# A dynamic convolution and two dense layers on one core: block 0 shared by heads, weights corrected on VectorE, boot order changed

## The chip, the cores and the metric

The kernel runs on 1 core of one Trainium2 chip. The metric is the device time of one execution in microseconds (us). It is given as the median of several runs; a profile is one further execution with its own time.

## What is computed

`x` is (2, 4096, 192) in f32, `weight_gen` is (2, 4096, 8 heads, 7 taps). The weights of the two dense layers are f64 numbers.

```python
w = softmax(weight_gen, axis=taps)                 # + 1e-9 in the sum
x_pad = six zero rows + x                          # per batch, along the sequence
a[b,s,h,g] = sum_k w[b,s,h,k] * x_pad[b,s+k,h,g]   # 8 heads x 24 columns
for (w_in, w_out), gate in ((moe, elu), (moe2, hardswish)):
    a = gate(a @ w_in) @ w_out                     # 192 -> 2048 -> 192, 8192 rows
```

## The kernel before, in words

The 8192 rows lie as 128 partitions of 64 positions. A **block** is four positions of every partition, 512 rows; there are 16, and each goes through both layers (m = 0 and 1). A **cell** (m, i, q) is one block and one eighth of the 2048 hidden columns. Cells run in one list, 256 of them, in a software pipeline: in step n, PE runs the first product of cell n (`first_product`) and the second product of cell n-3 (`second_product`), ACT the exponential (L494, L495) and the rounding to fp32r (L501), DVE the gate (L511, L514) and the rounding's remainder (L505). Every product is made of three, high by high, high by low and low by high, so weights and activations are each kept as a rounded high part and a low part. The two halves of the partitions (k = 0, 1) run as two streams of 64-row products on PE; a note on SP's queue tells one stream when the other has left a bank.

**Boot.** Cells 0 to 15 are blocks 0 and 1 of the first layer, in the order of `SPLIT`: columns 0 to 4 of both blocks, then 5 to 7 of both. While they run, the first layer's weights are made, in 16 **units** (class `Unit`), sorted by the cell that first needs them. Units 0 to 3, 5 and 10 to 12 are columns of the layer's first matrix (kind "i"), needed from cells 0, 1, 2, 3, 4, 10, 11, 12 on; units 4, 6 to 9 and 13 to 15 are rows of its second (kind "o"), needed in cells 3 to 7 and 13 to 15. The f64 words arrive in a raw buffer; `begin` (ACT, L150) and `s0` to `s3` (DVE, L154 to L169) build the f32 value `f` from the high word, `s4` (DVE, L182) the part from the low word, `high` (ACT, L175) the rounded weight. `p5` makes the low part on PE: identity times `f`, minus identity times the rounded weight, plus identity times the low word's part (L187 to L189), and `p6` (ACT, L194) evicts it. Units below 6 are `busy`: their steps work on a PSUM bank. The list `at` names the step in which a unit's DVE steps are issued, `high` follows one step later and `p5`, `p6` two. Unit n's raw buffers are asked for by `want` up to two units ahead. After the boot the second layer's units are made by `wst`.

**Convolution.** `attention(i)` gives the steps for block i: softmax (`s0` to `s2`, L246 to L272; DVE, the exponential on ACT) and seven products with six sums. For block 0 DVE takes positions 0 and 1 (its products and weights in PSUM) and GpSimd (POOL) positions 2 and 3; later blocks are POOL's alone. Six rows of halo ahead of each partition's positions come from the partition before, in two DMAs of 63 partitions (L226), requested after the first unit's weights, which `load_block` requests through `between`. `prepare` transposes the result on PE (L327, L331), casts it to its high part on ACT (L338), subtracts on DVE (L340), and copies halves of the partitions across by four DMAs (L345).

**The end of a block.** `fold_b` and `fold_a` collect the second product; blocks 0 and 1, whose columns are split, keep a first sum (`keep_b`) that DVE adds in `rest` (L369) before the halves are added (L373).

**DMAs.** All are issued on SP. `later` issues one at once or puts it on a list, `transfers` issues from that list behind the notes in `matmuls`; before cell 16 the list is emptied after every cell's products.

Of the kernel before, what the change touches and what calls it, by code (L numbers as in the profile page):

```python
# [17 lines left out]
def kernel(  # L18
# [26 lines left out]
    P = 128  # L45
# [29 lines left out]
    plus, minus = (cpool.tile([P, P], F32R, name=n) for n in ("plus", "minus"))  # L75
# [25 lines left out]
    def load_w(kind, m, q):  # L101
        raw = stage.tile([P, UN, 2], U32, tag="raw", name="raw", bufs=RAWS)
        if kind == "i":
            for k in range(2):
                c = (2 * q + k) * 2 * P
                src = w_in[m][:, c:c + 2 * P].rearrange("(g p) c -> p g c", p=HP)
                dst = raw[half[k]].rearrange("p (g c) b -> p g (c b)", g=3)
                if k == 0:
                    later(0, dst, src)
                else:  # L110
                    for s, g in enumerate((1, 0, 2)):
                        later(0, dst[:, s], src[:, g])
# [11 lines left out]
    class Unit:  # L124
# [52 lines left out]
        def s4(self):  # L177
            f = o = self.r.bitcast(F32)
            if self.m == 0:
                c = self.n % NQ * UN  # L180
                o = self.rr = bootr[:, c:c + UN]
            nc.vector.scalar_tensor_tensor(o, self.lw, 2.0**-52, f, op0=ALU.mult, op1=ALU.mult)  # L182

        def p5(self):

            hi, _, v = self.parts()
            nc.tensor.matmul(self.ps, ident, self.f.bitcast(F32), start=True, stop=False)  # L187
            nc.tensor.matmul(v(self.ps), minus, hi, start=False, stop=False)
            nc.tensor.matmul(self.ps, plus, self.rr, start=False, stop=True)  # L189
# [22 lines left out]
    def load_block(i, between=None):  # L212
        t0 = TM * i
        xt = xw.tile([P, TM + HALO, D], F32, tag="xt", name="xt", bufs=2)
        wt = xw.tile([P, TM * H, K], F32, tag="wt", name="wt", bufs=2)
        later(
            0, wt.rearrange("p a k -> p (a k)"), wv[:, t0:t0 + TM, :].rearrange("p t c -> p (t c)"))
        m = max(0, HALO - t0)
        later(0, xt[:, m:HALO + TM, :], xv[:, t0 - HALO + m:t0 + TM, :])
        if between:  # L220
            between()
        if m:

            for b in range(B):
                nc.gpsimd.memset(xt[b * PB:b * PB + 1, 0:m, :], 0.0)
                nc.sync.dma_start(  # L226
                    xt[b * PB + 1:(b + 1) * PB, 0:m, :],
                    xv[b * PB:(b + 1) * PB - 1, TP + t0 - HALO:TP + t0 - HALO + m, :])
        return xt, wt

    def attention(i):
# [6 lines left out]
        hn = n // 2  # L238
# [18 lines left out]

        if i == 0:

            pw = hset[1][0][:, 0:hn * K].rearrange("p (a k) -> p a k", k=K)  # L260
            po = hset[0][0][:, 0:2 * D].rearrange("p (t e) -> p t e", e=D)
            hs = [(nc.vector, slice(0, 2), pw, po), (nc.gpsimd, slice(2, 4), w3[:, hn:, :], tmp[:, 0:2])]
        else:
            hs = [(nc.gpsimd, slice(0, TM), w3, tmp)]

        def s2():
            s = tt["m"]
            if i == 0:
                v.tensor_tensor(pw, w3[:, :hn, :], s[:, :hn, :].to_broadcast([P, hn, K]), op=ALU.mult)
                v.tensor_tensor(w3[:, hn:, :], w3[:, hn:, :], s[:, hn:, :].to_broadcast([P, hn, K]), op=ALU.mult)  # L270
            else:
                v.tensor_tensor(w3, w3, s.to_broadcast(shp), op=ALU.mult)  # L272

        def product(k):
            def s():
                for eng, t, w, o in hs:
                    nt = t.stop - t.start
                    xk = xt[:, t.start + k:t.stop + k, :].rearrange("p t (h g) -> p t h g", g=G)
                    wk = w[:, :, k:k + 1].to_broadcast([P, nt * H, G])
                    if k == K - 1:  # L280
                        o = y[:, t, :]
                    eng.tensor_tensor(  # L282
                        o.rearrange("p t (h g) -> p t h g", g=G), xk,
                        wk.rearrange("p (t h) g -> p t h g", h=H), op=ALU.mult)
            return s

        def add():
            for eng, t, _, o in hs:
                eng.tensor_tensor(y[:, t, :], y[:, t, :], o, op=ALU.add)  # L289

        def add_a():
            for eng, t, _, o in hs:
                eng.tensor_tensor(y[:, t, 0:P], y[:, t, 0:P], o[:, :, 0:P], op=ALU.add)

        def add_d():

            for eng, t, _, o in hs:
                if t.stop - t.start == 2:
                    d = t.start // 2 * HP
                    eng.tensor_tensor(yd[:, :, d:d + HP], y[:, t, P:D], o[:, :, P:D], op=ALU.add)  # L300
                else:
                    v = lambda t: t.rearrange("p (a s) e -> p s a e", a=2)[..., P:D]
                    eng.tensor_tensor(yd.rearrange("p s (a e) -> p s a e", a=2), v(y), v(o), op=ALU.add)
# [11 lines left out]
    def prepare(m, i, parts=(0, 1)):  # L315
# [20 lines left out]
        def split():  # L336
# [6 lines left out]
            for k in "hl":  # L343
                for a in range(2):
                    later(first[m, i] == SPLIT if first[m, i] <= BOOT else 2, X[k][half[1 - a], 1].bitcast(F32), X[k][half[a], 0].bitcast(F32))  # L345
# [7 lines left out]
    def fold_b(m, i):  # L353
# [6 lines left out]
        if (m, i) in part:  # L360
            first_part = part.pop((m, i))
        else:
            first_part = None
# [3 lines left out]
        def rest():  # L367
            if first_part is not None:
                nc.vector.tensor_tensor(b, b, first_part, op=ALU.add)  # L369
# [42 lines left out]
    def first_product(n, k):  # L412
# [7 lines left out]
        for j, (w, x, s) in enumerate((  # L420
# [9 lines left out]
            c = q * UN + s * P  # L430
# [23 lines left out]
    def matmuls(n):  # L454
# [18 lines left out]
        for _, k, (o, w, r, st, sp, wait, tell) in sorted(plan, key=lambda e: e[:2]):  # L473
# [3 lines left out]
            if tell:  # L477
# [39 lines left out]
    RAWS, RB, YB = 4, 3, 1  # L517
# [4 lines left out]
    SPLIT = 5  # L522
    BOOT = EARLY = 2 * NQ
# [68 lines left out]
    def want(n):  # L592
        if n < len(units) and n not in made:
            u = made[n] = Unit(*units[n])
            u.n = n
            if n < BOOT:
                u.busy = n < 6

                u.bank = {1: acca[1], 2: accb, 3: acca[0], 5: acca[1]}.get(n, aux)

    def w_steps(n):
        def step(k):
            def s():
                if k < 0:
                    for a in range(3):
# [13 lines left out]
    with tc.manual_schedule():  # L619
# [5 lines left out]
        nc.scalar.mul(minus, ident, -1.0)  # L625
# [3 lines left out]
        for k in "aaaawwawawawaw":  # L629
# [15 lines left out]
        wst = Stream(wtasks)  # L645
        for n in range(len(cells) + LAG + 3):
# [49 lines left out]
            for i in range(2, NB):  # L696
# [13 lines left out]
            if n < BOOT:  # L710
# [33 lines left out]
```

## Time and profile before

| | |
|---|---|
| median of 3 runs | 1260.06 us (1259.47 to 1260.61) |
| the profiled execution | 1260.44 us |
| its span, first to last instruction | 1258.7 us |
| busy in the span | PE 1210.0, DVE 941.3, ACT 857.1, POOL 413.5 us |
| chain of work that ended last | PE 90%, DVE 5%, ACT 3%, DMA 1% |
| mean granted TensorE clock | 0.989 |

The span is shorter than the execution by what lies around it, 1.7 us. A busy time is a sum over the whole span; PE's matmuls are pipelined and their ends are modelled. Idle time of an engine is put down to what released it last. L345 is line 345 of the kernel above. In a timeline the first column is the start in us from the span's beginning, the second how long the instruction was on its engine; idle time before it stands in brackets with its releaser.

### The profile page before, as it was taken

Reading aid. Unit: us, or ns where it says so; the run is one execution under the profiler, and the core shown is the slowest. Engines: PE = TensorE matmul, PEld = TensorE weight load, DVE = VectorE, ACT = ScalarE, POOL = GpSimd, SP = SyncE. Lnnn points to the kernel's source line nnn. Section 1 sums busy time; section 2 is a strip of 40 time slices with the busy share of each in tenths; the row PEclk is TensorE's granted clock in tenths of the full one; section 3 lists DMA queues with packets and bytes.
Section 4 is the critical chain, followed back from the end, with each engine's and each line's share of the span. In section 5 each row is a group of like instructions: output and inputs, shape, how many; then the busy total and the mean of one; then the engine's idle time right before and its main releaser. Section 6 shows DMA issues by size and latency. Waiting matters only on the chain.

```text
span 1258.7 us, 25471 instructions
## 1 busy us (share of the span) xinstructions
PE 1210.0 (96%) x10176; PEld 1075.4 (85%) x10176; DVE 941.3 (75%) x1226; ACT 857.1 (68%) x1342; POOL 413.5 (33%) x234
## 2 busy tenths in 40 slices
PE   3997889999999999999999999999999999999998
PEld 2665778998999998999888888988888899999996
DVE  6879689899899999999777666666666666666663
ACT  2765678888888888888886565566656655666553
POOL 7425767777877777788000000000000000000000
PEclk9998989999999999999999999999999999999999
DMA  6341121122222212221111011111111111111110
GB/s 166 102 124 38 59 87 66 46 75 86 86 86 86 68 41 66 86 86 51 52 51 38 27 52 51 39 51 52 28 37 51 51 52 39 52 51 25 41 39 26
DMA packets 33686, 75.82 MB, mean 60 GB/s; under 512 B 4644, under 2 KB 17058, under 8 KB 33568
## 3 DMA queue, kind: packets, MB, share of 16 engines
q1 hardware_dynamic: 33568, 74.19, 20.2%
q8 instruction: 80, 1.31, 0.5%
q14 instruction: 38, 0.31, 0.1%
HBM read 36.43 MB, written 12.58 MB: 39 GB/s over the span
## 4 chain that ended last, share of the span: by engine, by line
PE 90%; DVE 5%; ACT 3%; DMA 1%; issue 1%; SPq 0%; DVEq 0%; ACTq 0%
PE h L474 41%; PE acca L474 28%; PE accb L474 19%; DVE gl L505 1%; ACT r L495 1%; ACT r L494 1%; DVE bootf L161 1%; DVE r L511 1%; DMA xt<-in_x_dram 1%; DMA xl<-xl 0%; DVE bootf L157 0%; DVE tr L169 0%; PE acca L327 0%; SPq L544 0%; DVE z L373 0%
## 5 line engine op out<-in xcount | busy, mean ns | idle before, releaser
L474 PE MATMUL h<-xh,wi_h 64*128 64x512 f32 x1536 | 574.2, 399 | 5.9 <-DVE r L511 3.2
L474 PE MATMUL h<-xh,wi_l 64*128 64x512 f32 x1536 | 574.8, 399 | 0.0
L474 PE MATMUL h<-xl,wi_h 64*128 64x512 f32 x1536 | 567.7, 398 | 2.0 <-DMA xl<-xl 2.0
L505 DVE TENSOR_TENSOR gl<-r,gh 128x1024 fp32r<-128x1024 f32 x256 | 374.8, 1464 | 64.7 <-ACT gh L501 61.7
L497 ACT ACTIVATE r<-h,three 128x512 f32<-128x512 f32 x256 | 176.6, 690 | 225.5 <-PE h L474 178.4
L474 PEld LDWEIGHTS h<-xh,wi_h 64*128 64x128 f32 x1536 | 287.1, 188 | 25.3 <-DVE r L511 4.9
L474 PEld LDWEIGHTS h<-xl,wi_h 64*128 64x128 f32 x1536 | 285.6, 188 | 19.4 <-DMA xl<-xl 3.0
L474 PEld LDWEIGHTS h<-xh,wi_l 64*128 64x128 f32 x1536 | 285.8, 188 | 16.7
L514 DVE SCALAR_TENSOR_TENSOR r<-r,h 128x512 f32<-128x512 f32 x256 | 176.1, 688 | 163.5 <-ACT r L497 162.6
L474 PE MATMUL acca<-gh,wo 64*128 64x512 f32 x1024 | 284.3, 397 | 0.0
L501 ACT CAST gh<-r 128x1024 fp32r<-128x1024 f32 x256 | 266.6, 1041 | 13.2 <-DVE r L511 12.4
L511 DVE SCALAR_TENSOR_TENSOR r<-r,h 128x512 f32<-128x512 f32 x256 | 174.1, 682 | 55.3 <-ACT r L495 54.6
L474 PEld LDWEIGHTS acca<-gh,wo 64*128 64x128 f32 x1024 | 191.5, 187 | 11.6
L282 POOL TENSOR_TENSOR tmp<-xt,wt 128x768 f32<-128x768 f32 (+1 forms) x96 | 188.8, 1966 | 7.4 <-DMA xt<-in_x_dram 1.2
L494 ACT ACTIVATE r<-h 128x512 f32<-128x512 f32 x256 | 152.7, 596 | 50.6 <-PE acca L474 26.9
L474 PE MATMUL accb<-gh,wo 64*128 64x512 f32 x512 | 165.6, 402 | 6.9 <-ACT wo L194 3.4
L495 ACT ACTIVATE r<-r 128x512 f32<-128x512 f32 x256 | 162.3, 634 | 8.1
L474 PE MATMUL accb<-gl,wo 64*128 64x512 f32 x512 | 163.0, 398 | 0.0
L474 PE MATMUL acca<-gl,wo 64*128 64x512 f32 x512 | 162.2, 396 | 0.0
L289 POOL TENSOR_TENSOR y<-y,tmp 128x768 f32<-128x768 f32 (+1 forms) x80 | 149.9, 1874 | 6.3
L474 PE MATMUL acca<-gh,wo1b 64*128 64x512 f32 x512 | 141.7, 396 | 0.3
L474 PE MATMUL acca<-gh,wo1a 64*128 64x512 f32 x512 | 140.3, 393 | 0.0
(143 smaller groups left out, 1850.3 us busy)
## 6 DMA issues: line engine op xcount, KB each, us to landing
xt<-in_x_dram SPq DMA_DIRECT2D x14, 960.0 KB, 5.4
xh<-xh SPq DMA_DIRECT2D x64, 192.0 KB, 2.7
xl<-xl SPq DMA_DIRECT2D x64, 192.0 KB, 2.9
raw<-in_moe_w_out_dram SPq DMA_DIRECT2D x16, 384.0 KB, 3.2
z<-z SPq DMA_DIRECT2D x16, 384.0 KB, 2.3
zin<-z SPq DMA_DIRECT2D x16, 384.0 KB, 3.0
out_dram<-ot SPq DMA_DIRECT2D x16, 384.0 KB, 2.3
raw<-in_moe_w_in_dram SPq DMA_DIRECT2D x16, 192.0 KB, 3.5
```

The source lines that it names most:

```text
L161: nc.vector.scalar_tensor_tensor(self.f, self.hw, 0xC0000000, self.b, op0=ALU.bitwise_and, op1=ALU.bitwise_or)
L282: eng.tensor_tensor(o.rearrange("p t (h g) -> p t h g", g=G), xk, wk.rearrange("p (t h) g -> p t h g", h=H), op=ALU.mult)
L289: eng.tensor_tensor(y[:, t, :], y[:, t, :], o, op=ALU.add)
L474: mm = nc.tensor.matmul(o, w, r, start=st, stop=sp).ins
L494: nc.scalar.activation(r, h, AF.Relu, scale=-1.0)
L495: nc.scalar.activation(r, r, AF.Exp, scale=-1.0)
L497: nc.scalar.activation(r, h, AF.Relu, bias=three)
L501: nc.scalar.copy(gg[n][0], rs[n])
L505: nc.vector.tensor_tensor(gl, rs.pop(n), gh.bitcast(F32), op=ALU.subtract)
L511: nc.vector.scalar_tensor_tensor(r, r, -1.0, h, op0=ALU.add, op1=ALU.max)
L514: nc.vector.scalar_tensor_tensor(r, r, 6.0, h, op0=ALU.min, op1=ALU.mult)
```

## The change

- `p5` has two products, both with the fp32r identity: one of `fl`, the other of the low word's part. `fl` is `f` minus the rounded weight, made by a new DVE step `left` one step after the unit's other DVE steps. The negative identity is gone. The low word's parts have four slots in place of eight, `fl` the other four.
- Block 0's convolution: DVE takes heads 0 to 4 of all four positions, POOL heads 5 to 7; POOL alone writes the last 64 columns.
- The halo's DMAs are issued before unit 0's weights. Block 0 is split (`prepare`) before the later softmax steps of block 1, not after them.
- Weight columns of the second half come in two DMAs in place of three, in another order, which `first_product` follows.
- `at` is written out: units 10 to 15 are made in steps 4, 5, 5, 6, 7, 8 in place of 5 to 10. Units 10 and 12 take the bank acca[1]. Raw buffers are five, and `want` looks three units ahead.
- From cell 3 on, DMAs of the boot go to the list and are issued up to three per cell behind the notes; the list is emptied at the ends of cells 0 to 2, 4 and 15. Block 1's half copies go to the front of the list, in turned order.
- The kept first sum is added in the step of `fold_b`, not in `fold_a`'s.

```diff
-    plus, minus = (cpool.tile([P, P], F32R, name=n) for n in ("plus", "minus"))
+    plus = cpool.tile([P, P], F32R, name="plus")
...
-                    for s, g in enumerate((1, 0, 2)):
-                        later(0, dst[:, s], src[:, g])
+                    later(0, dst[:, 0:2], src[:, 1:3])
+                    later(0, dst[:, 2], src[:, 0])
...
         def s4(self):
...
-                c = self.n % NQ * UN
+                c = self.n % 4 * UN
...
+                self.fl = bootr[:, c + 4 * UN:c + 5 * UN]
...
+        def left(self):
...
+            hi, _, v = self.parts()
+            nc.vector.tensor_tensor(v(self.fl), v(self.f.bitcast(F32)), hi.bitcast(F32), op=ALU.subtract)
...
         def p5(self):
...
-            hi, _, v = self.parts()
-            nc.tensor.matmul(self.ps, ident, self.f.bitcast(F32), start=True, stop=False)
-            nc.tensor.matmul(v(self.ps), minus, hi, start=False, stop=False)
+            nc.tensor.matmul(self.ps, plus, self.fl, start=True, stop=False)
...
-        if between:
-            between()
...
+        if between:
+            between()
...
-            pw = hset[1][0][:, 0:hn * K].rearrange("p (a k) -> p a k", k=K)
-            po = hset[0][0][:, 0:2 * D].rearrange("p (t e) -> p t e", e=D)
-            hs = [(nc.vector, slice(0, 2), pw, po), (nc.gpsimd, slice(2, 4), w3[:, hn:, :], tmp[:, 0:2])]
-        else:
-            hs = [(nc.gpsimd, slice(0, TM), w3, tmp)]
+            c = P // G
+            pw = hset[1][0][:, 0:TM * c * K].rearrange("p (t h k) -> p t h k", t=TM, k=K)
+            po = hset[0][0][:, 0:TM * c * G].rearrange("p (t h g) -> p t h g", t=TM, g=G)
+            hs = [(nc.vector, slice(0, c), pw, po), (nc.gpsimd, slice(c, H), w4[:, :, c:], th[:, :, c:])]
+        else:
+            hs = [(nc.gpsimd, slice(0, H), w4, th)]
+        yh = y.rearrange("p t (h g) -> p t h g", g=G)
...
          def product(k):
             def s():
+                for eng, h, w, o in hs:
+                    xk = xt[:, k:TM + k, :].rearrange("p t (h g) -> p t h g", g=G)[:, :, h]
+                    wk = w[:, :, :, k:k + 1].to_broadcast([P, TM, h.stop - h.start, G])
+                    eng.tensor_tensor(yh[:, :, h] if k == K - 1 else o, xk, wk, op=ALU.mult)
...
         def add_d():
...
+            v = lambda t: t.rearrange("p (a s) e -> p s a e", a=2)[..., P:D]
+            nc.gpsimd.tensor_tensor(yd.rearrange("p s (a e) -> p s a e", a=2), v(y), v(tmp), op=ALU.add)
...
-                    later(first[m, i] == SPLIT if first[m, i] <= BOOT else 2, X[k][half[1 - a], 1].bitcast(F32), X[k][half[a], 0].bitcast(F32))
+                    (later0 if first[m, i] <= BOOT else later)(2 - (first[m, i] == SPLIT), X[k][half[1 - a], 1].bitcast(F32), X[k][half[a], 0].bitcast(F32))
...
-            first_part = part.pop((m, i))
-        else:
-            first_part = None
+            p = part.pop((m, i))
+            jobs.append(lambda: nc.vector.tensor_tensor(b, b, p, op=ALU.add))
...
         def rest():
-            if first_part is not None:
-                nc.vector.tensor_tensor(b, b, first_part, op=ALU.add)
...
-            c = q * UN + s * P
+            c = q * UN + ((0, 2, 1)[s] if k else s) * P
...
-                if now >= BOOT and tell[1] == 1:
+                if now >= 3 and tell[1] == 1:
...
-        if now < BOOT:
+        if now < 3:
...
-    RAWS, RB, YB = 4, 3, 1
+    RAWS, RB, YB = 5, 3, 1
...
+    AT = (-3, -2, -1, 0, 0, 1, 1, 2, 3, 4, 4, 5, 5, 6, 7, 8)
...
-    now, waiting = None, []
+    now, waiting, jobs = None, [], []
...
-        if now is None or now >= len(cells) or now < BOOT and n == 0:
+        if now is None or now >= len(cells) or now < 3 and n == 0:
...
+    def later0(n, out, in_):
...
+        if now is None or n == 2:
+            nc.sync.dma_start(out, in_)
+        else:
+            waiting.insert(0, (now + n, out, in_))
...
-    at = []
-    for d, *_ in units:
-        at.append(min(d - 3, at[-1] + 1) if at else -3)
+    at = AT
+    assert all(a <= u[0] - 3 for a, u in zip(at, units))
...
-                u.bank = {1: acca[1], 2: accb, 3: acca[0], 5: acca[1]}.get(n, aux)
+                u.bank = {1: acca[1], 2: accb, 3: acca[0], 5: acca[1], 10: acca[1], 12: acca[1]}.get(n, aux)
...
     def w_steps(n):
         def step(k):
             def s():
...
-                    for a in range(3):
+                    for a in range(4):
...
-        for k in "aaaawwawawawaw":
+        for k in "aaaawwawawaw":
...
+        made[0].left()
...
-        for s in c1[:4]:
-            s()
-        prepare(0, 0)()
-        for s in c1[4:] + w_steps(1):
+        split = prepare(0, 0)
+        c1[0]()
+        split()
+        for s in c1[1:] + w_steps(1):
...
+        made[1].left()
...
+            for u in range(BOOT):
+                if at[u] == n - 1:
+                    made[u].left()
...
-            if n < BOOT:
+            if n < 3 or n == SPLIT - 1 or n == BOOT - 1:
...
```

## Rows read from the trace of the kernel before

**Rows 1.** Stages: us; busy PE, PEld, DVE, ACT, POOL; granted clock, DMA share, GB/s
```profile
23.70:50.00 26.30, 24.04 (x70) 16.28 (x70) 22.77 (x38) 16.12 (x31) 22.34 (x14) 1.00 0.58 172
50.00:86.70 36.70, 33.15 (x238) 24.45 (x240) 26.36 (x50) 26.79 (x51) 0.00 (x0) 1.00 0.36 105
86.70:127.10 40.40, 32.51 (x201) 22.45 (x200) 37.69 (x40) 22.29 (x42) 24.66 (x14) 0.87 0.17 55
127.10:171.50 44.40, 38.71 (x292) 31.44 (x294) 31.42 (x41) 27.12 (x44) 26.05 (x14) 0.88 0.13 41
171.50:1258.70 1087.20, 1078.45 (x9370) 978.91 (x9366) 808.41 (x1027) 759.46 (x1164) 324.01 (x168) 1.00 0.19 55
```

**Rows 2.** Timeline to cell 0: start, us, engine, line, operation [idle before <-releaser]
```profile
6.84 0.52 ACT L150 ACTIVATE aux<-raw 128x384 f32<-128x384 f32 x1 [2.50 <-DMA raw<-in_moe_w_in_dram]
...
12.02 0.56 DVE L282 TENSOR_TENSOR h<-xt,h 128x384 f32<-128x384 f32 x1 [3.13 <-DMA xt<-in_x_dram]
...
18.35 0.55 DVE L289 TENSOR_TENSOR y<-y,h 128x384 f32<-128x384 f32 x1
...
18.94 0.56 DVE L282 TENSOR_TENSOR h<-xt,h 128x384 f32<-128x384 f32 x1
...
19.87 0.28 DVE L300 TENSOR_TENSOR y<-y,h 128x128 f32<-128x128 f32 x1
...
20.21 0.69 PE L327 MATMUL h<-ident,y 64*128 64x64 f32 x8 [2.92 <-DVE y L300]
...
22.67 1.01 DVE L340 TENSOR_TENSOR xl<-h,xh 128x384 fp32r<-128x384 f32 x2
...
23.74 0.79 PE L474 MATMUL h<-xh,wi_h 64*128 64x512 f32 x1 [2.63 <-DVE xl L340]
```

**Rows 3.** Timeline of DVE, steps with SBUF operands alone
```profile
38.64 2.57 DVE L505 TENSOR_TENSOR gl<-r,gh 128x1024 fp32r<-128x1024 f32 x1
...
43.53 1.23 DVE L157 TENSOR_SCALAR bootf<-bootf 128x384 uint32<-128x384 uint32 x1
...
52.72 1.22 DVE L505 TENSOR_TENSOR gl<-r,gh 128x1024 fp32r<-128x1024 f32 x1
```

**Rows 4.** Timeline of DVE, end of block 2's softmax, unit 12, cell 9
```profile
86.30 0.39 DVE L272 TENSOR_TENSOR wt<-wt,mx 128x224 f32<-128x224 f32 x1
...
86.99 1.67 DVE L157 TENSOR_SCALAR bootf<-bootf 128x384 uint32<-128x384 uint32 x1
...
108.75 1.27 DVE L511 SCALAR_TENSOR_TENSOR r<-r,h 128x512 f32<-128x512 f32 x2
```

**Rows 5.** Busy time from 6 to 8 us (columns as above), and SP's queue
```profile
6.00:8.00 2.00, 0.00 (x0) 0.00 (x0) 0.61 (x2) 0.52 (x1) 1.83 (x3) 1.00 0.53 192
...
1.66 2.65 SPq L544 DMA_DIRECT2D raw<-in_moe_w_in_dram  x4
```

**Rows 6.** Timeline of PE, the correction products of unit 1
```profile
30.74 1.65 PE L187 MATMUL acca<-bootf,ident 128*128 128x384 f32 x2
...
32.51 0.52 PE L189 MATMUL acca<-bootr,plus 128*128 128x384 f32 x1
```

**Rows 7.** Timeline of DVE, first gate of cell 0
```profile
30.43 0.69 DVE L511 SCALAR_TENSOR_TENSOR r<-r,h 128x512 f32<-128x512 f32 x1 [1.05 <-ACT r L495]
```

**Rows 8.** Timeline of PE, start of cell 3 and wait in cell 5
```profile
50.03 0.50 PE L474 MATMUL accb<-gh,wo 64*128 64x512 f32 x1 [1.47 <-ACT wo L194]
...
67.29 0.49 PE L474 MATMUL h<-xl,wi_h 64*128 64x512 f32 x1 [1.20 <-DMA xl<-xl]
```

**Rows 9.** Timeline of PE, waits ahead of cells 11 and 13
```profile
105.65 1.65 PE L187 MATMUL aux<-bootf,ident 128*128 128x384 f32 x2 [3.28 <-ACT wi_l L194]
...
127.07 0.43 PE L327 MATMUL aux<-ident,y 64*128 64x64 f32 x4 [2.99 <-ACT wo L194]
```

**Rows 10.** Timeline of DVE and PE, fold of block 0
```profile
150.51 2.33 DVE L369 TENSOR_TENSOR fold<-fold,bootf 128x512 f32<-128x512 f32 x1
...
157.29 0.50 PE L474 MATMUL h<-xh,wi_h 64*128 64x512 f32 x1 [1.22 <-DVE r L511]
```

More of the change, by code (lines that the diff above doesn't have):

```diff
@@ L237, in attention @@
         v = nc.vector
-        hn = n // 2
         yt = xw.tile([P, 2 * N], F32, tag="y", name="y", bufs=YB)
@@ L256, in s1 @@
             v.reciprocal(s, s)
+        w4, th = w3.rearrange("p (t h) k -> p t h k", h=H), tmp.rearrange("p t (h g) -> p t h g", g=G)
         if i == 0:
-            pw = hset[1][0][:, 0:hn * K].rearrange("p (a k) -> p a k", k=K)
-            po = hset[0][0][:, 0:2 * D].rearrange("p (t e) -> p t e", e=D)
-            hs = [(nc.vector, slice(0, 2), pw, po), (nc.gpsimd, slice(2, 4), w3[:, hn:, :], tmp[:, 0:2])]
-        else:
-            hs = [(nc.gpsimd, slice(0, TM), w3, tmp)]
+            c = P // G
+            pw = hset[1][0][:, 0:TM * c * K].rearrange("p (t h k) -> p t h k", t=TM, k=K)
+            po = hset[0][0][:, 0:TM * c * G].rearrange("p (t h g) -> p t h g", t=TM, g=G)
+            hs = [(nc.vector, slice(0, c), pw, po), (nc.gpsimd, slice(c, H), w4[:, :, c:], th[:, :, c:])]
+        else:
+            hs = [(nc.gpsimd, slice(0, H), w4, th)]
+        yh = y.rearrange("p t (h g) -> p t h g", g=G)
         def s2():
@@ L268, in s2 @@
             if i == 0:
-                v.tensor_tensor(pw, w3[:, :hn, :], s[:, :hn, :].to_broadcast([P, hn, K]), op=ALU.mult)
-                v.tensor_tensor(w3[:, hn:, :], w3[:, hn:, :], s[:, hn:, :].to_broadcast([P, hn, K]), op=ALU.mult)
+                s4 = s.rearrange("p (t h) k -> p t h k", h=H)
+                for _, h, w, _ in hs:
+                    v.tensor_tensor(
+                        w, w4[:, :, h], s4[:, :, h].to_broadcast([P, TM, h.stop - h.start, K]), op=ALU.mult)
             else:
@@ L275, in s, with add_one @@
             def s():
[L276 to L284, printed above, removed]
+                for eng, h, w, o in hs:
+                    xk = xt[:, k:TM + k, :].rearrange("p t (h g) -> p t h g", g=G)[:, :, h]
+                    wk = w[:, :, :, k:k + 1].to_broadcast([P, TM, h.stop - h.start, G])
+                    eng.tensor_tensor(yh[:, :, h] if k == K - 1 else o, xk, wk, op=ALU.mult)
             return s
         def add():
-            for eng, t, _, o in hs:
-                eng.tensor_tensor(y[:, t, :], y[:, t, :], o, op=ALU.add)
+            for eng, h, _, o in hs:
+                eng.tensor_tensor(yh[:, :, h], yh[:, :, h], o, op=ALU.add)
         def add_a():
-            for eng, t, _, o in hs:
-                eng.tensor_tensor(y[:, t, 0:P], y[:, t, 0:P], o[:, :, 0:P], op=ALU.add)
-        def add_d():
[L297 to L300, printed above, removed]
-                else:
-                    v = lambda t: t.rearrange("p (a s) e -> p s a e", a=2)[..., P:D]
-                    eng.tensor_tensor(yd.rearrange("p s (a e) -> p s a e", a=2), v(y), v(o), op=ALU.add)
+            for eng, h, _, _ in hs:
+                if eng is nc.vector:
+                    add_one(eng, h, po)
+                else:
+                    c = slice(h.start * G, P)
+                    eng.tensor_tensor(y[:, :, c], y[:, :, c], tmp[:, :, c], op=ALU.add)
+        def add_one(eng, h, o):
+            eng.tensor_tensor(yh[:, :, h], yh[:, :, h], o, op=ALU.add)
+        def add_d():
+            v = lambda t: t.rearrange("p (a s) e -> p s a e", a=2)[..., P:D]
+            nc.gpsimd.tensor_tensor(yd.rearrange("p s (a e) -> p s a e", a=2), v(y), v(tmp), op=ALU.add)
         steps = [s0, s0e, s1, s2, product(K - 1)]
@@ L624 @@
         nc.scalar.copy(plus, ident)
-        nc.scalar.mul(minus, ident, -1.0)
         blk[1] = load_block(1)
         todo = {"w": w_steps(0), "a": attention(0)}
-        for k in "aaaawwawawawaw":
+        for k in "aaaawwawawaw":
             todo[k].pop(0)()
```

## Prediction, made before the change was run

> **What bounds the kernel now.** I read the clock first: one core, mean granted TensorE clock 0.989, so nearly all of it runs at 2.4 GHz. Then the table of busy time by stage [rows 1]. After 171.5 us TensorE (PE) is busy 1078.45 of 1087.20 us at clock 1.00; nothing in the change touches a cell after the sixteenth but the order of some columns, so this part stays. The case lies in the first 171.5 us. That stage holds 236 of the 256 cells, 4.6 us each; the first twenty, worth 92 us, take the 147.8 us from 23.74 [rows 2] to 171.5.
>
> Next the stages one by one. Between 23.7 and 50 VectorE (DVE) is busy 22.77 of 26.30 us and PE 24.04; between 86.7 and 127.1 DVE 37.69 of 40.40 and PE 32.51 at clock 0.87 [rows 1]. Between 50 and 86.7 DVE is busy only 26.36 of 36.70 us. So the boot is held by DVE's queue wherever GpSimd (POOL) works beside it, and by a PE-ScalarE (ACT) round in between. Why is seen in the timeline: the same 128x1024 subtraction of L505 takes 2.57 us beside POOL and 1.22 us without; a 128x384 step with only SBUF operands takes 1.23 us at 43.53 [rows 3] and 1.67 us at 86.99 [rows 4], while a step of that size with an operand in PSUM keeps 0.56 us beside POOL [rows 2].
>
> **Start, to the first cell.** The products of block 0 stop until 12.02 us for the halo (3.13 us idle), and end with L300 at 19.87 + 0.28 = 20.15; the transposes follow at 20.21 and cell 0 at 23.74 [rows 2]. The four weight DMAs occupy SP's queue 2.65 us from 1.66 [rows 5]; the change puts the two halo DMAs ahead of them, so the halo is asked for 2.65 us earlier. But the unit's first DVE step stands before product 6 in DVE's queue and needs the weights: ACT had them at 6.84 [rows 2], and from there to product 5 are ACT 0.5 and three DVE steps of about 0.5, 2.1 us. Bounds for product 5: 9.1 us (weights not delayed, 7.0 + 2.1) and 14.0 (weights land only when the halo did, 11.9 + 2.1). The 6 to 8 us row, 192 GB/s at 0.53 of the engines [rows 5], says the halo DMAs do not fill the engines, so some of the weights pass; I take 10.9, 1.1 earlier.
>
> From there 12 products and sums in place of 13 instructions: 480 elements by heads instead of 384. Their spacing is 0.59 us (18.35 to 18.94, [rows 2]), 0.40 of it streaming; 480 elements make it 0.69. That is +1.2, +0.9 after the last small sum and one weight step leave the chain. POOL, with 288 elements, ends about with it. Then comes a **new order**: s4 and the new subtraction (`left`) end after the products, 1.1 us, and PE's queue has unit 0's correction ahead of the transposes; with two products it takes about 0.85 us at 1.2 GHz (the third product of unit 1 has 0.52 us, and the three run from 30.74 to 33.0, 2.2 us, [rows 6]). Before, all this lay in the halo wait. +2.0. Splitting block 0 before block 1's softmax takes the latter out from between 20.15 and the subtraction at 22.67 [rows 2]: -1.0. Sum: -1.1 + 0.9 + 2.0 - 1.0 = +0.8 (bounds -1.0 and +3.9).
>
> **Cells 0 to 3.** PE saves 2.2 - 0.85 us per unit at half clock, but DVE sets the pace: block 1's softmax now delays units 1 and 2 by what it no longer delays cell 0, and p5 waits for `left` on DVE. Units 1 and 2 lose the 1.05 us hole at 30.43 [rows 7] to `left`; I get unit 3 started 0.9 later. `left` of units 3 and 4 has three SBUF operands (bootf, the rounded weights, bootr) and stands ahead of units 5 and 6. Nearest row: 1.23 us each in that very stretch [rows 3], 2.4; bounds 1.1 (twice 0.56, no POOL) and 3.3 (twice the 1.67 of 86.99). Cell 3 waits for unit 4's eviction (1.47 us at 50.03, [rows 8]) behind ACT's rounding of unit 6, which waits for DVE, so all of it arrives: +3.3. Queued behind are L505, the gates and PE's next first product. PE then stands some 5 us instead of 1.5; after 3.28 us of idleness at 105.65 it ran at 1.2 GHz for a cell [rows 9]. Bounds 0 and 2.5 (5 us at half clock); +1.5.
>
> **Cells 3 to 13.** Second-layer units are still made three cells ahead of use, so from cell 3 to 7 the round "matmuls end, ACT's Relu and Exp, eviction, next cell" stands, and the correction products, which PE runs while ACT does these, hide in it: 0. (Without that cover their shrinking would give 0.7 us a unit.) Block 1's half swap no longer comes after all notes of cell 4: the 1.20 us wait at 67.29 [rows 8] goes, but eight DMAs of 0.6 us are flushed on SP at the end of cell 4 and the next note stands behind them, +0.5. Two more units (five steps, some 2.3 us each by 1.22 us for 1024 elements, [rows 3]) and six `left` beside no POOL (0.56 each) go into DVE's 10.3 idle us of this stage [rows 1]; by their order, ACT's rounding in cell 6 is late, and softmax of block 2 ends (L272, 86.30 before, [rows 4]) 1.1 later altogether. There POOL starts block 2. **The units of cells 7 and 8 meet POOL as before**, only they are now the last two, with `left` of units 13 and 14 added and pushing the first step of each into the contention: 0.56 + 0.55 + two steps of 1.2 to 1.4 more, +3.6 at the gate that was at 108.75 [rows 4]. Unit 15's correction waits for its `left`, behind softmax of block 3: cell 11 starts about 67 us after cell 3 instead of 59.4 (109.4 - 50.0). In return cells 11 and 12 have no unit, no extra products, and the 2.99 us wait for aux at 127.07 [rows 9] is gone: an estimate of 7.5 (half of it at 1.2 GHz) + 4.9 us instead of the 17.9 from 109.4 to 127.3. So cell 13 comes 79.4 us after cell 3 instead of 77.3, with the 1.1 of above in it. Together +2.2 (bounds -4, if POOL's first operations let the two units pass, and +5).
>
> **Cells 13 to 20.** A mean clock of 0.88 over 44.4 us [rows 1] is some 10.7 us at 1.2 GHz; about 3 of them follow the wait for aux in cell 13, which then costs 1.4 us less: -1.4. The first part's sum of block 0 (L369, 2.33 us at 150.51) moves one cell forward, where DVE is as full, but ACT and the sums behind it no longer wait: -0.9 to -3 with PE's gap of 1.22 at 157.29 [rows 10] and the slow clock after it; I take -1.2. Other edits (a sixth less weight DMAs, a fifth raw buffer, paced transfers) cost nothing: what hides them is a cell of lead; without it, 0.6 us each.
>
> **Sum.** +0.8 + 3.3 + 1.5 + 2.2 - 1.4 - 1.2 = +5.2 us. The profiled execution took 1260.44 us (span 1258.7), 0.4 above the median 1260.06, so 1265.3 against the median; I give 1265.
>
> **A rule against the trace.** The Trainium skill, page "DMA: Bandwidth & Descriptors", section "Why a DMA increments its semaphore by 16 and not by 1", says that a DMA is spread over the largest number of engines up to 16 that divides its outer dimension: 63 partitions would use 9, and by "Queues, rings and completion order" each engine takes its descriptors in turn. The trace agrees so far: 0.53 of 16 engines is 8.5. By it the weights would stand behind the halo on those nine engines, product 5 would come at 12.5 to 14, and the sum would be about +7.5.
>
> **Rivals.** (a) *Weights last* (that rule as a mechanism): product 5 at 13.5 instead of 10.9, 1268; for it the 0.53, against it that the halo's own 7.7 us, from 4.3 to 12.02, were shared with block 1's loads, issued behind it; chance 0.14. (b) *DVE's holes take it* (faster): `left` costs 0.5 everywhere, since 3.5 us are idle between 23.7 and 50 and 10.3 between 50 and 86.7 [rows 1]; start -1.0, cells 0 to 3 -0.5, clock 0, cells 3 to 13 -2 (wait for aux and half-clock cells gone), end -1.4 and -2.5: -7.4, 1253. It decides if `left` stays below about 0.8 us beside POOL. Chance 0.36. (c) *It cancels*: the two late cells give back what the lefts took, within 2.5 us; chance 0.17. (d) My sum, 1265, chance 0.33. That `left` in place of a product does not change PE's bound at all is part of (c).
>
> **How the numbers follow.** About 0.2% (2.5 us) is what a measurement of this kernel can tell from no change. Slower: (a) and (d), 0.47; same 0.17; faster 0.36. Cases of both signs hold most of the chance: the slower ones alone reach 1263 to 1271; the range that leaves out 2 in 10 is 1251 to 1271.
>
> **What would show it.** Right: `left` over 1.1 us beside POOL before 50 us and near 0.56 after; cell 3 at 54 to 56 us; units 14 and 15 with steps of 1.7 to 1.9 us; no PE wait for aux before block 2's transposes. Wrong: cell 3 before 50 us, product 5 before 9.5 us, or cell 13 before 125 us; then (b) holds.

## The result, and the profile of the changed kernel

The changed kernel took 1267.13 us (three runs, 1266.43 to 1268.53), 1.0058 times the kernel before (interval 1.0035 to 1.0081). Five runs more (the base, below) gave 1266.78 us, 1.0044 times 21 runs of the kernel before (1.0032 to 1.0057). Executions of one kernel differ by as much as many effects below (the kernel before took 1259.29 to 1262.68 us in those 21), and a profile shows one of them. The profiled execution has a span of 1266.7 us, 8.0 more than before, at a mean granted clock of 0.981. Its stages, with the columns of [rows 1]:

```profile
23.70:50.00 26.30, 18.42 (x73) 12.12 (x73) 23.80 (x42) 13.66 (x26) 19.21 (x11) 0.87 0.55 160
50.00:86.70 36.70, 25.76 (x175) 19.90 (x176) 31.01 (x61) 23.98 (x48) 4.64 (x4) 0.81 0.29 77
86.70:127.10 40.40, 26.36 (x176) 18.87 (x176) 38.59 (x42) 20.73 (x41) 24.93 (x14) 0.85 0.21 67
...
180.00:1266.70 1086.70, 1078.07 (x9361) 994.87 (x9358) 807.59 (x1025) 757.70 (x1162) 323.63 (x168) 1.00 0.19 55
```

The last row is the last one of [rows 1] again, begun 8.5 us later and half a microsecond shorter: the steady part did not move. Ahead of it VectorE is busier in all three stages (31.01 us against 26.36 from 50 to 86.7) and TensorE idler (25.76 against 33.15).

The column of the clock needs care at the start. The trace has no record of the clock before 46.2 us in the kernel before and 36.6 us in the changed one, and the rows count that time as 1.00. The products tell otherwise: those of 512 columns that follow one another take 0.62 us there (24.33 before the change, 29.19 behind it), as they do where the record says 0.50 (126.36 behind it), and 0.39 us where it says 1.00 (137.03). Up to their first record both kernels ran at 1.2 GHz, so 1.00 against 0.87 in the stage from 23.7 to 50 us is not a loss of clock.

The start, from the timeline:

```profile
1.66 0.72 SPq L228 DMA_DIRECT2D xt<-in_x_dram  x2
2.42 2.08 SPq L548 DMA_DIRECT2D raw<-in_moe_w_in_dram  x3
...
11.49 0.69 POOL L288 TENSOR_TENSOR tmp<-xt,wt 128x288 f32<-128x288 f32 x1 [4.76 <-DMA xt<-in_x_dram]
...
13.18 0.51 ACT L150 ACTIVATE aux<-raw 128x384 f32<-128x384 f32 x1 [8.99 <-DMA raw<-in_moe_w_in_dram]
...
15.22 0.65 DVE L288 TENSOR_TENSOR h<-xt,h 128x480 f32<-128x480 f32 x1
...
25.14 0.69 PE L192 MATMUL aux<-bootr,plus 128*128 128x384 f32 x1 [25.14 <-DVE bootr L188]
...
28.60 0.79 PE L477 MATMUL h<-xh,wi_h 64*128 64x512 f32 x1 [1.62 <-DVE xl L346]
```

The halo, asked for 2.7 us earlier, is there 0.5 us earlier (11.49 against 12.02 in [rows 2]); unit 0's weights come 6.3 us later (13.18 against 6.84). Product 5 waits for both, and cell 0 starts 4.9 us late.

The semaphores in the trace show what held the weights. Each of the two halo DMAs raises its semaphore once when it is issued and nine times as it lands (6.16 to 8.28 and 9.53 to 11.36 us). Each of unit 0's three weight DMAs raises its own sixteen times: of the first, seven come at 7.26 to 7.83 us and nine at 10.10 to 12.13; of the last, seven at 8.91 to 9.41 and nine at 11.37 to 13.07. Nine of sixteen parts came some 2 us or more behind the other seven, as they would if the halo held nine engines of sixteen.

The new subtraction on VectorE with GpSimd's first operation of block 2, then TensorE where it stands longest:

```profile
35.49 1.59 DVE L188 TENSOR_TENSOR bootr<-bootf,wi_h 128x384 fp32r<-128x384 f32 x1
...
38.65 0.55 DVE L188 TENSOR_TENSOR bootr<-bootf,wi_h 128x384 fp32r<-128x384 f32 x1
...
46.34 0.99 DVE L188 TENSOR_TENSOR bootr<-bootf,wi_h 128x384 fp32r<-128x384 f32 x1
47.26 1.89 DVE L188 TENSOR_TENSOR bootr<-bootf,wo 128x384 fp32r<-128x384 f32 x1
...
96.76 0.55 DVE L188 TENSOR_TENSOR bootr<-bootf,wo 128x384 fp32r<-128x384 f32 x1
97.22 1.70 DVE L154 TENSOR_SCALAR bootf<-bootf 128x384 f32<-128x384 f32 x1
...
110.00 0.97 DVE L188 TENSOR_TENSOR bootr<-bootf,wo 128x384 fp32r<-128x384 f32 x1
...
124.17 0.55 DVE L188 TENSOR_TENSOR bootr<-bootf,wo 128x384 fp32r<-128x384 f32 x1
```

```profile
97.06 1.65 POOL L288 TENSOR_TENSOR y<-xt,wt 128x768 f32<-128x768 f32 x1 [42.26 <-issue]
```

```profile
45.25 0.79 PE L477 MATMUL h<-xh,wi_l 64*128 64x512 f32 x1 [2.90 <-ACT wi_l L198]
...
57.92 0.79 PE L477 MATMUL accb<-gh,wo 64*128 64x512 f32 x1 [6.29 <-ACT wo L198]
...
111.11 0.66 PE L192 MATMUL aux<-bootr,plus 128*128 128x384 f32 x1 [5.54 <-DVE bootr L188]
...
124.86 0.66 PE L192 MATMUL aux<-bootr,plus 128*128 128x384 f32 x1 [6.77 <-DVE bootr L188]
...
165.18 0.49 PE L477 MATMUL h<-xh,wi_h 64*128 64x512 f32 x1 [1.22 <-DVE r L514]
```

Cell 3 waits 6.29 us where it waited 1.47 [rows 8]; the corrections of units 14 and 15 wait for `left`. The wait for aux ahead of block 2's transposes [rows 9] is gone. The 1.22 us of [rows 10] are still there.

### The profile page after: what moved, and what is told of

It reads as the page before. It is cut to its first block, busy times and chain, and to the rows that moved or that the text cites. A ratio compares the mean times of both kernels' runs of the same rounds, so it can differ in the third digit from the quotient of the medians.

```text
span 1266.7 us, 25390 instructions
## 1 busy us (share of the span) xinstructions
PE 1195.5 (94%) x10144; PEld 1083.2 (86%) x10144; DVE 952.0 (75%) x1241; ACT 855.1 (68%) x1341; POOL 411.9 (33%) x234
## 4 chain that ended last, share of the span: by engine, by line
PE 89%; DVE 6%; ACT 2%; issue 1%; DMA 1%; SPq 1%; DVEq 0%; ACTq 0%
PE h L477 41%; PE acca L477 28%; PE accb L477 19%; DVE r L514 1%; DVE gl L508 1%; ACT r L498 1%; DMA raw<-in_moe_w_in_dram 1%; DVE bootf L161 1%; ACT r L497 1%; DVE bootr L188 1%; DVE bootf L154 0%; SPq L564 0%; DVE z L376 0%; DVE tr L169 0%; PE acca L333 0%
## 5 line engine op out<-in xcount | busy, mean ns | idle before, releaser
L477 PE MATMUL h<-xh,wi_h 64*128 64x512 f32 x1536 | 581.2, 399 | 4.2 <-DVE r L514 2.2
L477 PE MATMUL h<-xh,wi_l 64*128 64x512 f32 x1536 | 581.1, 399 | 2.9 <-ACT wi_l L198 2.9
L477 PE MATMUL h<-xl,wi_h 64*128 64x512 f32 x1536 | 573.8, 397 | 1.0 <-DMA xl<-xl 1.0
L293 POOL TENSOR_TENSOR y<-y,tmp 128x768 f32<-128x768 f32 (+1 forms) x80 | 147.0, 1837 | 6.3
```

The lines of the kernel that those rows point to most:

```text
L293: eng.tensor_tensor(yh[:, :, h], yh[:, :, h], o, op=ALU.add)
L477: mm = nc.tensor.matmul(o, w, r, start=st, stop=sp).ins
```

## The experiments

The kernel before was timed again beside them, on the same chips. Its median was 1261.56 us beside "weights first", "no `left`", "the old order" and "halves by positions"; 1261.43 beside the base, the two runs with the halo in pieces and "the softmax put back"; 1261.18 beside "unit 0's steps", "three products late" and "the order alone"; 1262.08 beside "`left` in the middle". The table gives lateness against the kernel before, in us, of cell 0's first product on TensorE, of the first gate of four cells on VectorE, and of the end of the span. Each row is one profile:

| kernel | cell 0 | gate 3 | gate 7 | gate 9 | gate 13 | end |
|---|---|---|---|---|---|---|
| before, at | 23.74 | 54.68 | 84.06 | 108.75 | 133.59 | 1258.7 |
| changed | 4.9 | 10.5 | 10.5 | 13.4 | 7.8 | 8.0 |
| changed, second profile | 3.6 | 8.5 | 8.5 | 11.4 | 6.8 | 7.3 |
| weights first | 2.5 | 6.9 | 6.9 | 9.8 | 4.9 | 3.3 |
| no `left` | 4.9 | 8.9 | 9.2 | 10.8 | 3.5 | 4.1 |
| old order | 2.6 | 7.2 | 5.7 | 8.8 | 6.2 | 5.9 |
| three products late | 3.1 | 7.6 | 7.6 | 7.5 | 0.1 | 0.1 |
| before, halo in pieces | -1.6 | -1.6 | -1.6 | -1.6 | -1.6 | -1.9 |
| the same, unit 0's steps early | -2.0 | -0.5 | -0.5 | -0.5 | -0.5 | -0.5 |
| order alone | -1.8 | 0.0 | 0.2 | 1.9 | -5.3 | -4.7 |
| `left` in the middle | -2.0 | 0.6 | 0.7 | 0.6 | -6.8 | -6.5 |

**The base.** The changed kernel again, unedited.

> The changed kernel itself, as the base for the runs beside it: 1266 to 1269 us, 5 to 8 above the kernel before.

Measured: 1266.78 us, 5.4 above the kernel before. Here unit 0's weights were there at 11.88 us and product 5 came at 13.93; over seven profiles of kernels with these first requests the weights came at 10.95 to 13.18.

**Weights first.** The call of `between` back ahead of the halo's DMAs:

```diff
         later(0, xt[:, m:HALO + TM, :], xv[:, t0 - HALO + m:t0 + TM, :])
+        if between:
+            between()
...
-        if between:
-            between()
         return xt, wt
```

> The changed kernel with one thing undone: unit 0's weights are requested ahead of the halo again. Theory (the weights behind the halo hold DVE's queue at the start): ACT has the weights at about 7 us instead of 13.2, product 5 starts at 11.5 to 12.3 us instead of 15.2 and waits for the halo, cell 0 starts 2.5 to 3.5 us earlier than 28.6, and the time falls from 1267.1 to 1263 to 1265. Rival (the new subtraction and the unit order make the loss, the start is swallowed later): cell 0 is earlier but cell 3 stays at 57 to 58 us, and the time stays at 1266 to 1267.5.

Measured: 1264.08 us, ratio 1.0025 (1.0016 to 1.0034), some 2.8 us of the 5.4 back. From its timeline, weights, then product 5, then cell 0:

```profile
7.30 0.51 ACT L150 ACTIVATE aux<-raw 128x384 f32<-128x384 f32 x1 [3.12 <-DMA raw<-in_moe_w_in_dram]
...
12.40 0.66 DVE L288 TENSOR_TENSOR h<-xt,h 128x480 f32<-128x480 f32 x1 [2.96 <-DMA xt<-in_x_dram]
...
26.24 0.79 PE L477 MATMUL h<-xh,wi_h 64*128 64x512 f32 x1 [1.62 <-DVE xl L346]
```

The halo, asked for 2 us later than in the changed kernel (3.75 against 1.66), holds product 5 until 12.40, within 0.4 of before. So the reordering bought little and delayed the weights.

**The halo in pieces.** Each DMA of 63 partitions cut in two, in the changed kernel and in the kernel before:

```diff
-                nc.sync.dma_start(xt[b * PB + 1:(b + 1) * PB, 0:m, :], ...)
+                for lo, hi in ((1, 49), (49, PB)):
+                    nc.sync.dma_start(xt[b * PB + lo:b * PB + hi, 0:m, :], ...)
```

> The changed kernel with each of the two halo DMAs of 63 partitions cut into one of 48 and one of 15 (two DMAs more, some 0.8 us more of SyncE's queue). Theory (the 63 partitions run on few DMA engines, the share was 0.53 while they ran alone, and unit 0's weights stand behind them there): share of the engines above 0.8 from 6 to 10 us, unit 0's weights at 10 to 11.5 us instead of 13.15, product 5 at 12.5 to 13.7 instead of 15.22, cell 0 1.5 to 2.7 us earlier, time 1.5 to 3 us less. Rival (the bytes set it: what is queued by then, block 1's included, takes that long on any engines): weights still at 12.5 to 13.5, time within 1 us of the changed kernel.

> The kernel before with each halo DMA of 63 partitions cut into one of 48 and one of 15, behind unit 0's weights as it was. By the theory of few engines the halo lands at 9.5 to 10.5 us instead of 11.9, product 5 follows at about 10 instead of 12.02, cell 0 comes 1 to 2 us earlier and the time is 1258.0 to 1259.3. By the rival (bytes) the halo lands at 11.5 to 12.5 as before and the time is within 0.7 us of the kernel before.

Measured: 1264.13 us for the changed kernel, ratio 1.0021 (1.0012 to 1.0030); 1258.81 for the kernel before, ratio 0.9988 (0.9979 to 0.9997), which beats it by some 1.5 us. (The 2.6 us of a later expectation are the difference of the medians.) In the first the weights were used at 10.04 us and cell 0 came at 25.47. Of the second, the stage of [rows 5] and product 5:

```profile
6.00:8.00 2.00, 0.00 (x0) 0.00 (x0) 0.88 (x2) 0.51 (x1) 1.84 (x3) 1.00 0.90 216
```

```profile
10.32 0.56 DVE L283 TENSOR_TENSOR h<-xt,h 128x384 f32<-128x384 f32 x1 [1.71 <-DMA xt<-in_x_dram]
```

The engines' share rose from 0.53 to 0.90 and the halo came 1.7 us earlier, with the same bytes. All cells moved by the same 1.6 us (the table). The rival of bytes alone falls. The semaphores agree: each of the four pieces in the kernel before raises its own sixteen times, one of them at issue for a piece of 15. No cut into other sizes was run.

**No `left`.** The three products of before and their negative identity, on everything else of the change:

```diff
-            nc.tensor.matmul(self.ps, plus, self.fl, start=True, stop=False)
+            nc.tensor.matmul(self.ps, ident, self.f.bitcast(F32), start=True, stop=False)
+            nc.tensor.matmul(v(self.ps), minus, hi, start=False, stop=False)
```

> The changed kernel with the three products of before in place of the new DVE subtraction. Theory (left beside POOL holds units 5 and 6 up before cell 3): the two subtractions at 46.3 and 47.3 us (2.7 us together) and the one at 35.5 (1.5) go, cell 3 starts 2 to 3 us earlier than 57.9, units 14 and 15 lose the pushed steps, but PE has 1.4 us more per unit at 1.2 GHz and unit 0's correction ahead of the transposes is 1.4 longer; the time is 1263 to 1266. Rival 1 (left is the whole loss): 1260 to 1261. Rival 2 (left is free, PE's shorter correction is a gain): 1268 to 1272.

Measured: 1262.65 us, ratio 1.0008 (0.9998 to 1.0019): 4.3 us back, more than the theory had. But cells 0 to 3 still took 28.5 us (28.62 to 57.12; 29.3 with `left`, 26.3 before): only 0.8 of the 3.0 is `left`'s. Of the 3.9 us by which this profile ends ahead of the changed kernel's, 1.4 are there at gate 7, and the other two thirds come behind it.

**Three products late.** The same for units 13, 14 and 15 alone (`if self.n >= 13`), the others with `left`.

> The changed kernel with `left` and two products for units 0 to 12 only; units 13, 14 and 15 (the ones that TensorE waited 5.5 and 6.8 us for) have the three products of before and no `left`. Theory (of the 4.3 us that the kernel without any `left` won, most lies in cells 8 to 13, where the gates went from 11.9 late to 7.8 late with `left` and from 10.8 to 3.5 without): 1263 to 1264.5, gates up to cell 7 as in the changed kernel, cell 13 2 to 3.5 us earlier against cell 7. Rival (the early lefts beside GpSimd's block 1 cost it): 1265.5 to 1267, cell 13 against cell 7 within 1 us of the changed kernel.

Measured: 1261.29 us, ratio 1.0001 (0.9992 to 1.0009). This alone gives back the whole loss, more than the theory had; whether it beats taking `left` away everywhere the times don't tell (the intervals overlap). Gate 9 against gate 7 is 0.1 earlier instead of 2.9 later. VectorE there, and GpSimd's first operation of block 2:

```profile
93.55 0.38 DVE L288 TENSOR_TENSOR wt<-wt,mx 128x224 f32<-128x224 f32 x1
94.15 0.36 DVE L154 TENSOR_SCALAR bootf<-bootf 128x384 f32<-128x384 f32 x1 [0.21 <-ACT bootf L150]
```

```profile
94.16 1.76 POOL L295 TENSOR_TENSOR y<-xt,wt 128x768 f32<-128x768 f32 x1 [41.12 <-issue]
```

In the changed kernel a `left` of 0.55 us stands between these two steps (96.76 above), the first step of unit 14 comes behind GpSimd's start (97.06) and takes 1.70 us instead of 0.36, and the two waits of 5.5 and 6.8 us follow. Here one wait is left, of 3.34 us ahead of 113.17.

The step's place is not all of it. With no `left` at all that step came behind GpSimd's start too, because ScalarE's `begin` was late:

```profile
96.47 1.36 DVE L154 TENSOR_SCALAR bootf<-bootf 128x384 f32<-128x384 f32 x1 [0.62 <-ACT bootf L150]
```

```profile
96.07 1.54 POOL L289 TENSOR_TENSOR y<-xt,wt 128x768 f32<-128x768 f32 x1 [42.08 <-PE acca L194]
```

There gates 7 to 9 lost 1.6 us, yet from gate 7 to gate 13 it won 5.7 us on the kernel before, where this kernel wins 7.5 and the changed one 2.8. So of the 4.7 us between the last two, at most some 1.8 go with the step's place. The other 2.9 go with the rest of the late `left`s: their own time (0.97 us at 110.00) and TensorE's waits for them.

**The softmax put back.** Block 1's softmax ahead of block 0's split:

```diff
-        split = prepare(0, 0)
-        c1[0]()
-        split()
-        for s in c1[1:] + w_steps(1):
+        for s in c1[:4]:
+            s()
+        prepare(0, 0)()
+        for s in c1[4:] + w_steps(1):
```

> The changed kernel with the softmax of block 1 back ahead of block 0's transposes and split (the first four steps together, as before). Without `left` at all, cells 0 to 3 were still 2.2 us longer than before (28.62 to 57.12 against 23.74 to 50.03), so `left` is not all of that term. Theory: the four softmax steps behind the subtraction (1.3 us of VectorE, 28.46 to 29.8) push units 1 to 4 back, and start GpSimd's block 1 later against the cells (30.1, 1.5 after cell 0, instead of 22.97, 0.8 ahead of it). Put back, cell 0 comes at 28.4 to 28.9 (28.60 in the changed kernel), cells 0 to 3 take 27 to 27.8 us instead of 29.3, and the time falls by 1 to 2.5 us. Rival (cells 0 to 3 are held by `left` beside GpSimd and the eviction before cell 3 alone, and the softmax finds holes): within 0.5 us of the changed kernel, cells 0 to 3 still 29 us or more.

Measured: 1266.58 us, ratio 1.0038 (1.0025 to 1.0051): not to be told from the base. Cells 0 to 3 took 27.9 us (27.65 to 55.51), 1.5 less, as the theory had it; but with the weights only 0.4 us earlier, cell 0 came 0.35 later than in the base. Put behind, the softmax gave cell 0 some 0.8 us and took 1.5 from the cells after it.

**The old order, and halves by positions.** The changed kernel with the old list of starts and banks, and with the old convolution:

```diff
-    at = AT
+    at = []
+    for d, *_ in units:
+        at.append(min(d - 3, at[-1] + 1) if at else -3)
```

> The changed kernel with the unit order of before (units 10 to 15 in steps 5 to 10, their low parts in the bank aux). Theory (two units meet POOL's block 2 either way, the order is worth little): 1266 to 1269, with a wait for aux of 2 to 3 us before block 2's transposes again. Rival (the new order is a gain that hides a larger loss elsewhere): 1270 to 1274. Rival (the new order is itself the loss): 1261 to 1264.

> The changed kernel with block 0's convolution divided by positions again (DVE 384 elements, POOL 384). Theory (the halves by heads cost 0.1 us more on each of 12 DVE steps and POOL had time to spare): cell 0 starts 0.8 to 1.3 us earlier than 28.6, the time is 1265.5 to 1266.5. Rival (POOL ends last when it takes half): cell 0 not earlier, 1267 to 1268.

Measured: 1266.88 us, ratio 1.0044 (1.0032 to 1.0056), and 1266.72, ratio 1.0037 (1.0025 to 1.0049). Neither is told from the base by its time. With the old order the wait for aux is back (1.94 us at 134.81), and units 12 and 13 lose beside GpSimd what 14 and 15 lose in the new one (3.1 us from gate 7 to 9). Halves by positions did bring product 5 to cell 0 in 12.2 us (14.08 to 26.32) instead of 13.4. That the order is worth nothing holds only beside the late `left`, as the next ones show.

**Unit 0's steps in the halo's wait,** on the kernel before in pieces:

```diff
-        for k in "aaaawwawawawaw":
+        for k in "aaaawwawwww":
```

> The kernel before with the halo in pieces of 48 and 15 partitions (alone: 2.6 us faster than the kernel before, and 1.6 us earlier in every cell from the first to the last), and unit 0's steps s1 to s4 all ahead of product 5, in VectorE's wait for the halo (1.7 us idle ahead of 10.32). Three of these steps, 0.46 us apart, leave the stretch between product 5 and the last sum. If VectorE's chain sets cell 0: cell 0 at 20.7 to 21.3 us (22.15 with the pieces alone), time 1257.0 to 1258.0. If GpSimd's half sets it (its last sum ends within some 0.3 us of VectorE's): cell 0 at 21.6 to 22.2 and less than 0.5 us won.

Measured: 1260.04 us, ratio 0.9988 (0.9979 to 0.9997), no better than the pieces alone. Cell 0 came at 21.75, 0.4 earlier: VectorE's half ends at 18.05 now and GpSimd's at 19.2, as the second case of the expectation had it. In this profile TensorE then stands longer ahead of cell 3 and is at 1.2 GHz for a part of it; the wait, and the stage behind it:

```profile
48.02 0.50 PE L475 MATMUL accb<-gh,wo 64*128 64x512 f32 x1 [4.38 <-ACT wo L194]
```

```profile
48.00:51.00 3.00, 2.98 (x18) 2.41 (x20) 2.78 (x7) 1.97 (x3) 0.00 (x0) 0.64 0.03 8
```

With the pieces alone the wait is 1.49 us and the clock 1.00 there; gate 3 is 1.6 us early with them and 0.5 here. By their times the two kernels are not told apart, and each profile is one execution, so it isn't shown that the earlier start made TensorE wait.

**The order alone.** The kernel before with pieces and early steps, plus the new starts, banks, fifth buffer, paced transfers, two weight DMAs in place of three and moved fold; no `left`, no halves by heads, halo behind the weights, softmax where it was.

> The respread units, fifth raw buffer, paced transfers and the moved fold alone, on the kernel before's convolution, softmax order and three products, with the weights ahead of the halo, the halo in pieces of 48 and 15 and unit 0's steps ahead of product 5. Theory: without `left` the new order is worth something: in the kernel without `left` the gates went from 8.9 us late in cell 3 to 3.0 late in cell 20, and the start and cells 0 to 3 are those of the kernel before here. Start -1.6 to -2.8, cells 0 to 3 within 1, cells 3 to 20 -2 to -5: 1253 to 1257.5, faster than either kernel and than the pieces alone. Rival (the late cells only caught up what the early ones had lost, and the order is worth nothing): the same as the kernel before with pieces and early steps, 1257 to 1259.

Measured: 1254.13 us, ratio 0.9942 (0.9928 to 0.9955), faster than both kernels. The gain is between gates 9 and 13, from 1.9 late to 5.3 early. Cells 0 to 3 took 28.1 us (21.98 to 50.03), longer than expected, but gate 3 was on time.

**`left` in the middle.** That kernel, with `left` and two products for units 5 to 12:

```diff
+            if not 5 <= self.n < 13:
+                return
             hi, _, v = self.parts()
             nc.vector.tensor_tensor(v(self.fl), ...)
```

> The kernel of the order alone (1254.13 us), with `left` and two products for units 5 to 12 only, which are made while GpSimd rests; the other units keep three products. Theory (of the three `left` groups only the middle one pays: where units 13 to 15 alone lost it, the gates went from 7.6 late in cell 7 to 0.1 late in cell 13, a gain of 7.5, and with no `left` at all the gain of that stretch was 5.7 there and 5.5 in the order alone): cells 3 to 7 within 1 us of the order alone, cells 7 to 13 up to 2 us shorter, 1251.5 to 1253.5. Rival (in the middle `left` is as idle as the product that it replaces): 1253.5 to 1255.5, cells 7 to 13 as in the order alone.

Measured: 1252.73 us, ratio 0.9926 (0.9913 to 0.9940). By the times it can't be told from the order alone (the intervals overlap); by the gates, 7 to 13 is 2.0 us shorter and the rest within 1, as the theory had it. The first step of unit 14, and GpSimd's start, of the order alone and then of this kernel:

```profile
87.55 1.36 DVE L154 TENSOR_SCALAR bootf<-bootf 128x384 f32<-128x384 f32 x1 [0.62 <-ACT bootf L150]
```

```profile
87.15 1.55 POOL L288 TENSOR_TENSOR y<-xt,wt 128x768 f32<-128x768 f32 x1 [42.24 <-PE acca L194]
```

```profile
87.24 0.36 DVE L154 TENSOR_SCALAR bootf<-bootf 128x384 f32<-128x384 f32 x1 [0.21 <-ACT bootf L150]
```

```profile
87.25 1.76 POOL L294 TENSOR_TENSOR y<-xt,wt 128x768 f32<-128x768 f32 x1 [42.36 <-issue]
```

Here that step is 0.01 us ahead of GpSimd instead of 0.4 behind it, and gates 7 to 9 lose nothing where they lost 1.6: nearly the whole 2.0 us. ScalarE's `begin`, for which it waited 0.62 us, is no longer late; that TensorE's shorter corrections of units 10 to 12 did this is likely, but it was not run apart.

## Why the prediction was right, and where its steps failed

The side and the range held, and so did the size: +5.2 forecast, +7.1 between the first medians, +5.4 in the second set. The signs to look for held but for two: cell 3 came at 57.9 us, not 54 to 56, by the late start, and of the four `left`s beside GpSimd before 50 us two took under 1.1 (0.55 and 0.99; the others 1.59 and 1.89). Of the steps, in the first profile (with the second in brackets):

- **Start, +0.8 forecast, +4.9 (+3.6) measured.** The step that failed is "some of the weights pass; I take 10.9": product 5 came at 15.22 (13.93). Of each weight DMA seven parts of sixteen did pass, but ScalarE began at 13.18, behind the last part (13.07). The first profile is past the step's upper bound too, 14.0, which let the weights land with the halo; they came 1.7 us behind it. That is rival (a), which had 13.5. By the rule that I set beside it, of the Trainium skill, page "DMA: Bandwidth & Descriptors", section "Why a DMA increments its semaphore by 16 and not by 1", 48 partitions would use 16 engines and 15 would use 15, where 63 use 9. The trace agrees: nine landings, and a share of 0.53 that became 0.90. The rest of the step held: product 5 to cell 0 grew by 1.7 us (11.72 to 13.38), forecast 1.9.
- **Cells 0 to 3, +3.3; +3.0 (+3.1).** Right in sum, wrong in its make-up. `left` was as slow as forecast (units 3 and 4: 0.99 + 1.89 = 2.88 us, forecast 2.4), but without it the stretch was only 0.8 shorter, as other steps then met GpSimd: there the first step of unit 6 took 1.94 us (1.50 with `left`) and the 128x1024 subtraction 2.19 (1.47). The softmax, which I had priced at 1.0 on either side of cell 0, gave 0.8 ahead of it and took 1.5 behind.
- **Half clock, +1.5; +2.6 (+1.9),** from cell 3's start (+7.9, +6.6) to its gate (+10.5, +8.5). The term was sized too small, past its bound of 2.5. From cell 3's start the granted clock stayed at 0.50 for 5.9 us (4.2), where before the change it was 1.00, and 2.6 (1.9) us is 0.44 (0.45) of that. The long wait ahead of cell 3 is not what brought it down in the first profile: the clock went to 0.50 at 43.4 us, in the wait of 2.90 us that ends at 45.25, and had not risen since. In the second it fell at 50.6, in a wait of 7.57 us ahead of cell 3.
- **Cells 3 to 13, +2.2; -1.1 (0.0),** from gate 3 to cell 13's first product (127.29 before; 136.69, 135.72). The parts came as forecast: units 14 and 15 met GpSimd (gates 7 to 9 lost 2.9, forecast 3.6), cell 11 started 67.9 (67.1) us after cell 3, forecast 67, and cell 13 another 10.9 (12.0) later, forecast 12.4. So cell 13 came 78.8 (79.1) us after cell 3, forecast 79.4. What failed is the sum: these 79.4 us begin at cell 3's start and, as measured, have the slow clock behind it in them, which I had added as a term of its own. The two terms together were forecast at +3.7 and came to +1.5 (+1.8).
- **Cell 13, -1.4; -1.7 (-1.7).** It held: from its first product to its gate it took 6.30 us before, with the clock at 0.50 from 128.1 to 131.5, and 4.65 (4.64) now.
- **The fold, -1.2; +0.3 (+0.6),** from gate 13 to the end. This step failed: TensorE's stalls around the fold are 1.22, 0.94 and 2.74 us where they were 1.22, 0.93 and 2.53, so the sum moved one cell forward shows no gain there (it was not run alone).

The measured terms sum to 4.9 + 3.0 + 2.6 - 1.1 - 1.7 + 0.3 = 8.0, the lateness at the end. The forecast came near it in part by luck: the start was 4.1 us too small, and the terms from cell 3 to 13 together 2.2 too large. Rival (b), VectorE's holes, is right for units 5 to 12, whose `left` takes 0.49 to 0.55 us. It is wrong for the last three, though theirs take hardly more (0.55, 0.97 and 0.55): what they cost lies in the steps that they push behind GpSimd's start and in TensorE's waits for them. Shown by runs: the start's cause, the late `left`s, the softmax's 1.5. Not separated: which of the new starts, banks, buffer, pacing, weight DMAs and fold makes the order's gain, and the last 0.7 us of cells 0 to 3. One profile is a weak witness there: the order alone and `left` in the middle run the same steps on VectorE up to cell 3 and took 28.1 and 26.3 us for these cells, with the first step of unit 6 at 1.69 us behind GpSimd's operation in one and 0.34 in the other.

## What to carry to other kernels

Look at the number of partitions of a DMA before its place in the queue: here 48 + 15 instead of 63 won what asking earlier could not, and asking earlier delayed what stood behind. Price work that is moved to an idle engine unit by unit, by what starts beside it: the same 0.55 us step cost nothing in the middle, and three of them cost 5 us at the end, where one pushed a unit's steps behind GpSimd's start and TensorE waited for the others. A part that shows no worth in one combination (the order beside the late `left`) may be the best of the change in another.

## What was not expected of the hardware

The weights' arrival, with the same requests in the same order, varied by 2.2 us over seven profiles (10.95 to 13.18), as much as several terms of the sum. And four profiles with nearly the same start, cell 0 at 21.75 to 22.15 us, went two ways. The two at 21.75 stood 4.38 and 4.16 us ahead of cell 3 and ran it in part at 1.2 GHz; the later two (21.98 and 22.15) stood less than 1.5 us and ran it at 1.00. Gate 3 came at 54.2 and 55.3 us in the first two, at 54.7 and 53.1 in the others. That the earlier start is the cause isn't shown: each is one execution.
